# A gated complex recurrence and a low-rank mixer: every engine's order taken from a list plan, blocks of 8 scaled to a middle token, the angle carried by a one-row DMA

## The chip, the cores and the metric

The kernel runs on one core of one Trainium2 chip. The metric is the device time of one execution in microseconds (us); lower is better. The engines are TensorE (PE, with its weight loads as PEld), VectorE (DVE), ScalarE (ACT), GpSimd (POOL), and SyncE (SP), which only starts transfers here.

## The reference

Inputs are q, k, v, a_re, a_im of shape (4 batches, 8 heads, 768 tokens, 48). Cut to what matters:

```python
mag = sqrt(a_re**2 + a_im**2); scale = minimum(mag, 0.999) / (mag + 1e-6)
for t in range(S):                       # complex state S_re, S_im: 48 x 48 per head
    new_re = ar*S_re - ai*S_im ; new_im = ar*S_im + ai*S_re
    S_re, S_im = new_re + outer(k[t], v[t]), new_im
    y[t] = q[t] @ S_re
x  = y as (batch, token, head*48 = 384)
u  = x + (x^T @ U @ V)^T                 # U: 768 x 32, V: 32 x 768, mixes tokens of one batch
out = u + relu(u @ w_ch1) @ w_ch2        # 384 -> 1536 -> 384
```

The gate of a token is a complex number per channel. The kernel keeps its magnitude as a logarithm and its angle as a number of turns. A product of gates over a range of tokens is then the exponential of a sum of logarithms, with a rotation by the sum of angles. U, V, w_ch1 and w_ch2 arrive as 64-bit floats.

## The kernel before

Each batch is cut into 6 chunks of 128 tokens (24 chunks in all, i = 0 to 23). The recurrence of a chunk becomes matrix products, and a 96 x 48 state `G` per head goes from chunk to chunk. The work of a chunk has four parts.

- **Gates** (`gate_steps`, for groups of one chunk, one chunk, and then two chunks each). ACT and DVE compute the logarithm `l` and the turns `y` in wide steps, with two ACT table loads in a group (L281, L323). PE sums them with constant 0/1 matrices: `es` (L301, matrix `after`) is the sum from a token to the end of its block of 4 tokens, `tot` (L314) has the totals of blocks of 4 to 128 tokens, and `ph` (L336) is the running angle of the chunk. The angle at the end of the chunk before is added by a second matmul into the same `ph` tile (L338), whose matrix `tail` picks the last row of `F`. `F` (L339, L340) is the angle with whole turns taken off. The temporaries have one buffer each, so the groups follow one another.
- **Prep** (`prep_steps`): q and k are scaled by `es`, rotated by `cs` (DVE), transposed by PE (`turn`, L380) and copied by ACT to `QK` (L382).
- **Chain** (`chain_steps`): the scores of a chunk are built from small blocks to large ones. `inner(n, hf)` (L417) makes 64 small matmuls inside blocks of 32 tokens, and a masked DVE copy (L421) keeps the pairs that belong to level n. `grow(hf)` multiplies q of each upper half and k of each lower half by the block's total, in place in `QK` (the DVE row of L256, 96 x 1024). `upper` is a half-size step of that kind. There are four `inner` steps: n = 5 (in a block of 4), n = 2 (4 to 8), n = 1 (8 to 16), n = 0 (16 to 32). Then follow `place`, `corners`, `corner`, `keys`, `outputs`, `state` and `rows_of_y` (L507 writes the chunk's x).
- **Mixer** (`mixer_steps`, 12 of them, two chunks each): `rank` (L548) needs all six x tiles of a batch, and with it no mixer can start before the last chunk of its batch. Then come `mixed` and `uT` (L558 to L564), twelve `up` steps (L571, relu by ACT) and two `down` steps (L579), a DVE add (L582) and the store, started by POOL (L583). The tiles `uT` and `h` have one buffer, x has eight.

The weights are turned from 64 to 32 bits by seven DVE steps for each piece (`single`, L211 to L221), 13 pieces.

The order before comes from the program: `weave` spreads several streams of steps evenly over a chunk's iteration: the end of the chain of chunk i-1, the levels of chunk i, the prep of chunk i+1, the gates of a later group, weight pieces, and a share of the mixer steps of earlier batches. Only ACT's table users (`tact`) and a few weight steps are tied to one another by extra edges (`behind`). The last batch's three mixers run one after another at the end:

```python
    weave((0.0, 1.0, rest), (0.0, 1.0, first[done:]))
    for m in range((NT - NCH) // MC, NT // MC):
        run(mixer_steps(m, pu))
```

Of the kernel before, what the change touches and what calls it, by code (L numbers as in the profile page):

```python
# [24 lines left out]
def weave(*streams):  # L25
    order = []
    for si, (begin, end, steps) in enumerate(streams):
        n = len(steps)
        for i, step in enumerate(steps):
            order.append((begin + (end - begin) * (i + 0.5) / n, si, i, step))  # L30
    for _, _, _, step in sorted(order, key=lambda e: e[:3]):
        step()
# [3 lines left out]
def kernel(  # L36
# [39 lines left out]
    M2LO, M2HI = 1e-16, 2.0 ** 62  # L76
# [7 lines left out]
    NTOT = FIRST[CH] + 1  # L84

    def pool(name, bufs, **kw):
        return ctx.enter_context(tc.tile_pool(name=name, bufs=bufs, **kw))

    singles = pool("singles", 1)
    pa = pool("pa", 1)  # L90
    pt = pool("pt", 1)
    pg = pool("pg", 2)
    pqk = pool("pqk", 2)
    pks = pool("pks", 1)
    pkc = pool("pkc", 1)
    pe = pool("pe", 3)
    pTT = pool("pTT", 6)
    pQK = pool("pQK", 3)
    pG = pool("pG", 2)
    py = pool("py", 1)  # L100
    px = pool("px", 8)
    psT = pool("psT", 2, space=PSUM)
    psA = pool("psA", 2, space=PSUM)
    psY = pool("psY", 2, space=PSUM)
    psM = pool("psM", 2, space=PSUM)

    T = {}
# [8 lines left out]
    def load_a(g):  # L116
        lo, hi = GROUPS[g]
        for nm, src in (("ar", a_re), ("ai", a_im)):
            t = pa.tile([128, GC, H, D], FP, tag=nm, name=nm)
            for i in range(lo, hi):  # L120
                nc.sync.dma_start(out=t[:, i - lo], in_=rows(src, i))
            T[nm, g] = t.rearrange("p c h d -> p (c h d)")[:, 0:(hi - lo) * DM]

    def load_qkv(i):
        T["qk", i] = pqk.tile([128, 2, H, D], FP, tag="qk", name="qk")
        for u, src in enumerate((q, k)):
            nc.sync.dma_start(out=T["qk", i][:, u], in_=rows(src, i))
        nc.sync.dma_start(out=VP[i % 4][:, :, 0:D], in_=rows(v, i))

    load_a(0)  # L130

    prefix = singles.tile([128, CH], FP, name="prefix")
    nc.sync.dma_start(out=prefix, in_=spans[:, PRE * CH:(PRE + 1) * CH])
    mask = singles.tile([128, 6, BLK], I32, name="mask")
    nc.sync.dma_start(out=mask, in_=masks)
    ident = singles.tile([128, 128], FP, name="ident")
    make_identity(nc, ident)
    quarter = singles.tile([128, 1], FP, name="quarter")
    nc.vector.memset(quarter, math.pi / 2)
    def column(nm, value):  # L140
# [5 lines left out]
    magic, fourth = column("magic", MAGIC), column("fourth", 0.25)  # L146

    tail = singles.tile([128, CH], FP, name="tail")
    nc.gpsimd.tensor_scalar(out=tail, in0=ident[:, 127:128].to_broadcast([128, CH]), scalar1=-1.0, scalar2=None,
                            op0=OP.mult)  # L150

    after = singles.tile([128, CH], FP, name="after")
    quads = prefix.rearrange("p (b t) -> p b t", t=4)
    nc.gpsimd.tensor_tensor(out=after.rearrange("p (b t) -> p b t", t=4),
                            in0=quads[:, :, 3:4].to_broadcast([128, CH // 4, 4]), in1=quads, op=OP.subtract)
    total = singles.tile([128, NTOT], FP, name="total")
    for n in SIZES:
        o, m, ends = FIRST[n], CH // n, prefix.rearrange("p (b t) -> p b t", t=n)[:, :, n - 1]
        nc.gpsimd.tensor_copy(out=total[:, o:o + 1], in_=ends[:, 0:1])
        if m > 1:  # L160
            nc.gpsimd.tensor_tensor(out=total[:, o + 1:o + m], in0=ends[:, 1:m], in1=ends[:, 0:m - 1], op=OP.subtract)

    for n in (3, 4):
        nc.vector.tensor_tensor(out=mask[:, 5], in0=mask[:, 5], in1=mask[:, n], op=OP.bitwise_or)
    F = singles.tile([128, GC, DM], FP, name="F")
# [10 lines left out]
    load_qkv(0)  # L176
    w1 = singles.tile([128, KD, FF], FP, name="w1")
    w2 = singles.tile([128, KF, DM], FP, name="w2")

    UV = singles.tile([128, 2 * NCH * R], FP, name="UV")  # L180
    U = UV[:, 0:NCH * R].rearrange("p (c r) -> p c r", r=R)

    V = singles.tile([128, S], FP, name="V")
    NP = 128 // R
    WP = 768

    def behind(ins, first):

        tc.add_manual_dep(ins.ins, first.ins.name, mybir.DependencyInfo(
            mybir.DependencyClass.NoSync, mybir.DependencyReason.DATA), reason="order")  # L190

    def single(st, o, pieces):


        n = o.shape[1]
        at = 0
        if pieces[0].dtype == FP:
            for i in pieces:
                nc.sync.dma_start(out=o[:, at:at + i.shape[1]], in_=i)
                at += i.shape[1]  # L200
            return
        raw = st[0].tile([128, WP, 2], U32, tag="raw", name="raw")[:, 0:n]
        for i in pieces:
            m = i.shape[1]
            nc.sync.dma_start(out=raw[:, at:at + m], in_=i.bitcast(U32).rearrange("p (m two) -> p m two", two=2))
            at += m
        lo, hi = raw[:, :, 0], raw[:, :, 1]
        x = st[1].tile([128, WP], U32, tag="x", name="cx")[:, 0:n]
        b = o.bitcast(U32)

        ins = nc.vector.tensor_scalar(out=x, in0=hi, scalar1=0x7FFFFFFF, scalar2=None, op0=OP.bitwise_and)  # L211
        if "level" in T:
            behind(ins, T["level"])
        xf = x.bitcast(FP)
        nc.vector.tensor_scalar(out=xf, in0=xf, scalar1=2.0 ** -15, scalar2=None, op0=OP.max)
        nc.vector.tensor_scalar(out=x, in0=x, scalar1=0x07FFFFFF, scalar2=3, op0=OP.bitwise_and,
                                op1=OP.logical_shift_left)
        nc.vector.scalar_tensor_tensor(out=b, in0=hi, scalar=0xC0000000, in1=x, op0=OP.bitwise_and, op1=OP.bitwise_or)
        nc.vector.tensor_scalar(out=x, in0=b, scalar1=0xFF800000, scalar2=None, op0=OP.bitwise_and)
        nc.vector.scalar_tensor_tensor(out=xf, in0=lo, scalar=2.0 ** -52, in1=xf, op0=OP.mult, op1=OP.mult)  # L220
        nc.vector.tensor_tensor(out=o, in0=o, in1=xf, op=OP.add)  # L221

    def weight_steps(st):
        def small():
            m = R * S // 128
            single(st, UV, [moe_U[c * 128:(c + 1) * 128] for c in range(NCH)] +
                   [moe_V.rearrange("r (s m) -> (r s) m", m=m)])
            for n in range(NP):
                nc.sync.dma_start(out=V[n * R:(n + 1) * R].rearrange("r (s m) -> r s m", m=m), in_=UV[:, NCH * R:])

        first, second = [small], []
        for m in range(0, FF, WP):
            for f in range(KD):
                (second if m else first).append(lambda f=f, m=m: single(
                    st, w1[:, f, m:m + WP], [moe_w_ch1[f * 128:(f + 1) * 128, m:m + WP]]))
        for f in range(0, KF, 2):
            second.append(lambda f=f: single(st, w2[:, f:f + 2].rearrange("p f m -> p (f m)"),
                                             [moe_w_ch2[e * 128:(e + 1) * 128] for e in (f, f + 1)]))
        return first, second

    def act(o, i, f, **kw):
        return nc.scalar.activation(out=o, in_=i, func=f, **kw)  # L242

    queued = []

    def queue(ins):

        if queued:
            behind(ins, queued[-1])
        queued[:] = [ins]  # L250

    def tact(*a, **kw):
        queue(act(*a, **kw))

    def mul(o, a, b):
        nc.vector.tensor_tensor(out=o, in0=a, in1=b, op=OP.mult)  # L256

    def heads(a):
        return a.rearrange("p (x d) -> p x d", d=D)

    def gate_steps(g):
        st = {}
        lo, hi = GROUPS[g]
        W = (hi - lo) * DM

        def tmp(nm):
            st[nm] = pt.tile([128, GC * DM], FP, tag=nm, name=nm)[:, 0:W]  # L270
            return st[nm]

        def s0():
            x, y = tmp("x"), tmp("y")
            act(x, T["ar", g], AF.Square)
            act(y, T["ai", g], AF.Square)
            nc.vector.tensor_tensor(out=x, in0=x, in1=y, op=OP.add)
            nc.vector.tensor_scalar(out=x, in0=x, scalar1=M2LO, scalar2=M2HI, op0=OP.max, op1=OP.min)
# [27 lines left out]
        def of_blocks(i):  # L306
# [3 lines left out]
            if g == 0:  # L310
                queue(nc.scalar.preload_act_table_set("natural_log_exp_and_others"))
# [288 lines left out]
    def run(steps):  # L600
        for f in steps:
            f()
# [97 lines left out]
```

## Time and profile before

| | |
|---|---|
| median of 3 runs | 874.59 us (873.63 to 874.9) |
| the profiled execution, its own time | 874.89 us |
| span of the profiled execution | 873.1 us |
| granted TensorE clock, mean | 0.96 |
| busy: PE / PEld / DVE / ACT / POOL | 788.9 / 585.5 / 426.0 / 464.7 / 37.7 us |

The span runs from the first to the last instruction; the profiled execution's own time is 1.8 us longer. Busy times are unions over the span. A matmul in fp32 appears as two instructions, and matmuls overlap, so the sum over PE's groups is above PE's busy time. The line L256 is the helper `mul`, which many steps use: its rows are told apart by their tiles and shapes.

### The profile page before, as it was taken

Reading aid. Unit: us, or ns where it says so; the run is one execution under the profiler, and the core shown is the slowest. Engines: PE = TensorE matmul, PEld = TensorE weight load, DVE = VectorE, ACT = ScalarE, POOL = GpSimd, SP = SyncE. Lnnn points to the kernel's source line nnn. Section 1 sums busy time; section 2 is a strip of 40 time slices with the busy share of each in tenths; the row PEclk is TensorE's granted clock in tenths of the full one; section 3 lists DMA queues with packets and bytes.
Section 4 is the critical chain, followed back from the end, with each engine's and each line's share of the span. In section 5 each row is a group of like instructions: output and inputs, shape, how many; then the busy total and the mean of one; then the engine's idle time right before and its main releaser. Section 6 shows DMA issues by size and latency. Waiting matters only on the chain.

```text
span 873.1 us, 24512 instructions
## 1 busy us (share of the span) xinstructions
PE 788.9 (90%) x11088; PEld 585.5 (67%) x11088; DVE 426.0 (49%) x621; ACT 464.7 (53%) x983; POOL 37.7 (4%) x67
## 2 busy tenths in 40 slices
PE   3657878878999999999999999999999999999997
PEld 2444656756767876866867867856868778576774
DVE  3577778798965635425526517417516343101010
ACT  7797887476754745736727729619614324020110
POOL 3000000010000000000000000000000000000000
PEclk9977989698799999999999999999999999999999
DMA  7431334243411401301301302301100000000000
GB/s 170 110 92 34 86 75 93 74 99 112 101 20 29 84 11 30 73 20 30 65 11 38 66 10 47 63 23 21 29 19 12 3 20 2 19 1 18 10 10 18
DMA packets 130904, 40.27 MB, mean 46 GB/s; under 512 B 126448, under 2 KB 127344, under 8 KB 130800
## 3 DMA queue, kind: packets, MB, share of 16 engines
q1 hardware_dynamic: 129264, 33.99, 17.6%
q0 software_dynamic: 1536, 4.72, 1.5%
q8 instruction: 87, 1.43, 0.7%
q14 instruction: 17, 0.14, 0.1%
HBM read 33.59 MB, written 4.72 MB: 44 GB/s over the span
## 4 chain that ended last, share of the span: by engine, by line
PE 71%; ACT 19%; DVE 5%; issue 3%; DMA 1%; POOL 1%; POOLq 0%; DVEq 0%; ACTq 0%
PE down L579 21%; PE up L571 18%; PE inner L417 5%; PE tot L314 4%; PE yT L473 4%; PE tr L380 3%; PE ph L336 2%; PE yT L477 2%; PE dk L493 2%; ACT y L242 2%; PE es L301 2%; ACT x L242 2%; ACT cs L242 2%; PE ks L487 2%; ACT AT L445 2%
## 5 line engine op out<-in xcount | busy, mean ns | idle before, releaser
L571 PE MATMUL up<-uT,w 128*128 128x256 f32 x864 | 211.8, 391 | 5.8 <-DVE uT L564 3.4
L579 PE MATMUL down<-w,h 128*128 128x384 f32 x576 | 190.2, 487 | 0.0
L256 DVE TENSOR_TENSOR QK<-QK,T 96x1024 f32<-96x1024 f32 (+1 forms) x144 | 157.1, 1095 | 49.4 <-PE corners L451 33.1
L571 PEld LDWEIGHTS up<-uT,w 128*128 128x128 f32 x864 | 159.8, 193 | 30.3 <-ACT h L242 5.1
L579 PEld LDWEIGHTS down<-w,h 128*128 128x128 f32 x576 | 108.1, 190 | 71.3 <-issue 0.2
L582 DVE TENSOR_TENSOR x<-down,x 128x384 f32<-128x384 f32 x24 | 13.4, 558 | 218.4 <-PE down L579 218.4
L242 ACT ACTIVATE h<-up 128x256 f32<-128x256 f32 x144 | 55.1, 383 | 118.6 <-PE up L571 118.1
L382 ACT COPY QK<-tr 96x512 f32<-96x512 f32 x96 | 55.6, 581 | 72.3 <-PE tr L380 71.4
L417 PEld LDWEIGHTS inner<-QK 96*32 96x32 f32 x6144 | 67.1, 114 | 33.0 <-issue 17.0
L417 PE MATMUL inner<-QK 96*32 96x16 f32 (+1 forms) x6144 | 79.5, 192 | 8.0 <-ACT AT L454 2.9
L380 PE MATMUL tr<-ident,qkc 128*96 128x128 f32 x384 | 63.2, 294 | 12.0 <-DVE qkc L256 10.8
L380 PEld LDWEIGHTS tr<-ident,qkc 128*96 128x96 f32 x384 | 43.9, 134 | 27.6 <-DVE qkc L256 8.8
L480 ACT COPY yTs<-yT 128x512 f32<-128x512 f32 x24 | 14.1, 586 | 82.7 <-PE yT L477 81.3
L421 DVE COPY_PREDICATED DG<-mask,inner 128x256 f32<-128x256 int32 (+1 forms) x96 | 31.6, 329 | 46.1 <-PE inner L417 44.8
L473 PE MATMUL yT<-AT,VP 128*64 128x128 f32 x384 | 46.6, 302 | 5.6 <-ACT AT L465 4.1
L256 DVE TENSOR_TENSOR qkc<-qk,cs 128x768 f32<-128x768 f32 x48 | 44.3, 947 | 2.3 <-PE tr L380 1.6
L445 ACT COPY AT<-DG 32x256 f32<-32x256 f32 x96 | 38.5, 401 | 9.6 <-DVE DG L421 8.7
L314 PEld LDWEIGHTS tot<-total,ll 128*96 128x96 f32 x384 | 37.8, 174 | 6.8 <-ACT ll L309 2.6
L314 PE MATMUL tot<-total,ll 128*96 128x63 f32 x384 | 39.2, 258 | 3.3 <-ACT ll L309 2.0
L473 PEld LDWEIGHTS yT<-AT,VP 128*64 128x64 f32 x384 | 29.6, 149 | 14.2 <-issue 8.1
L301 PE MATMUL es<-l,after 128*128 128x384 f32 x48 | 24.7, 606 | 14.5 <-DVE l L291 12.7
L477 PE MATMUL yT<-QK,G 96*48 96x128 f32 x320 | 37.6, 295 | 0.0
(93 smaller groups left out, 931.4 us busy)
## 6 DMA issues: line engine op xcount, KB each, us to landing
ar<-in_a_re_dram SPq DMA_DIRECT2D x24, 192.0 KB, 3.1
ai<-in_a_im_dram SPq DMA_DIRECT2D x24, 192.0 KB, 3.4
qk<-in_q_dram SPq DMA_DIRECT2D x24, 192.0 KB, 2.9
qk<-in_k_dram SPq DMA_DIRECT2D x24, 192.0 KB, 3.5
VP<-in_v_dram SPq DMA_DIRECT2D x24, 192.0 KB, 2.6
raw<-in_moe_w_ch_dram SPq DMA_DIRECT2D x6, 768.0 KB, 4.8
raw<-in_moe_w_ch_dram SPq DMA_DIRECT2D x12, 384.0 KB, 3.5
out_dram<-x POOLq DMA_DIRECT2D x24, 192.0 KB, 2.1
```

Source lines behind the costliest of these rows:

```text
L242: return nc.scalar.activation(out=o, in_=i, func=f, **kw)
L256: nc.vector.tensor_tensor(out=o, in0=a, in1=b, op=OP.mult)
L301: nc.tensor.matmul(out=ps, lhsT=after, rhs=st["l"][:, (i - lo) * DM:(i - lo + 1) * DM], start=True, stop=True)
L314: nc.tensor.matmul(out=ps[0:D2, h, 0:NTOT], lhsT=ll[:, h].rearrange("p u d -> p (u d)"), rhs=total, start=True, stop=True)
L380: nc.tensor.transpose(out=ps[0:D2, j], in_=T["qkc", i][:, u, hh * HH + j].rearrange("p u d -> p (u d)"), identity=ident)
L382: nc.scalar.copy(out=T["QK", i][:, u, hh * HH:(hh + 1) * HH], in_=ps[0:D2])
L417: nc.tensor.matmul(out=ps[js, h], lhsT=k_of(h)[:, js], rhs=part(q_of(h)[:, js], "p"), start=True, stop=True, tile_position=(0, j * BLK))
L445: nc.scalar.copy(out=AT[i % 2][js, :, js], in_=DG[i % 2][js])
L473: nc.tensor.matmul(out=y[u * DP:(u + 1) * DP, p], lhsT=vv[:, h], rhs=AT[i % 2][:, h], start=True, stop=(c == 0), tile_position=(0, u * DP))
L477: nc.tensor.matmul(out=y[u * DP:u * DP + D, p], lhsT=T["G"][:, h], rhs=q_of(h), start=False, stop=True, tile_position=(0, u * DP))
L571: nc.tensor.matmul(out=ps, lhsT=w1[:, f, ff * 128:(ff + 1) * 128], rhs=st["uT"][:, f], start=(f == 0), stop=(f == KD - 1))
L579: nc.tensor.matmul(out=ps, lhsT=st["h"][:, ff, cc * CH:(cc + 1) * CH], rhs=w2[:, ff], start=(ff == 0), stop=(ff == KF - 1))
```

## The change

Three things change together.

1. **The order.** Steps no longer run when they are written. Each one is given to a `Plan` with its engine, an estimated cost, a rank, what it reads and what it writes. `Plan.order()` simulates the five engines: whenever an engine is free, it takes the ready step with the lowest rank whose buffers are to be had. The instructions are then issued in that order, and at the end every instruction is tied behind the one before it on its engine. The edges order and do not signal. PE steps are handed over in smaller pieces: `inner`, `tot`, `outputs`, `dk` in two, `down` in six of four instructions. Ranks are chunk numbers with offsets; `up` and `down` stand last on PE (100 + m), while the other mixer steps and the ACT and DVE work of the mixers stand first (-5). `rank`, `mixed` and `uT` take their PSUM buffers from the pool of `es`, `tot`, `ph`, `tr` now.
2. **Blocks of 8.** `es` is scaled to the fourth token of a block of 8 (matrix `mid` in place of `after`), so the pairs of a whole block of 8 come from one `inner` step. The step n = 2 goes, with its masked copy. `grow(4)` and the half-size `upper` become two full-size multiplications (`times`).
3. **The angle carry.** The matmul with `tail` goes. POOL starts a DMA that adds the last row of the earlier `F` to the first row of `y`, before the `ph` matmul. `F` has two buffers for groups now, and the sign of `F` is turned.

The core of the diff (the weights, loads, gates' wide steps and mixer steps are the same operations, given to the plan):

```diff
-def weave(*streams):
+class Plan:
+    def add(self, engine, cost, rank, f, reads=(), writes=(), late=0.0):
+        ...   # needs: the earlier steps that touch the same tiles, one of them as a writer
+    def order(self):
+        ...
+            for e in free:
+                kept = []
+                while free[e] <= now and ready[e]:
+                    r = heapq.heappop(ready[e])      # lowest rank first
+                    n = r[1]
+                    if not fits(n):                  # no buffer free for its tiles
+                        kept.append(r)
+                        continue
+                    ...
+                    free[e] = now + ops[n][1]
+                    heapq.heappush(events, (free[e], n, 0))
+                    heapq.heappush(events, (free[e] + ops[n][2] + self.lag, n, 1))
+    plan = Plan(0.06)
+    def c_act(n):
+        return 0.22 + 0.0008 * n
+    def c_dve(n):
+        return 0.15 + 0.00104 * n
+    def SP(*a, **kw):
+        plan.add("SP", *a, late=2.0, **kw)
...
+        POOL(0.5, -7, lambda: nc.gpsimd.tensor_tensor(
+            out=mid..., in0=e[:, :, 3:4].to_broadcast([128, CH // 8, 8]), in1=e, op=OP.subtract), ...)
...
-            if not first:
-                nc.tensor.matmul(out=ps, lhsT=tail, rhs=F[:, (i - 1) % GC], start=False, stop=True)
+            if where(i)[1] > 0:
+                POOL(0.55, R2, lambda: nc.gpsimd.dma_start(out=of(y, i)[0:1], in_=fo(i - 1)[CH - 1:CH], accum_op=OP.add),
+                     [("F", group_of(i - 1), i - 1)], [yi], late=1.6)
...
-        add(inner, 5, 2)
-        add(grow, 4)
-        add(inner, 2, 4)
-        add(upper)
-        for n, hf in ((1, 8), (0, 16)):
-            add(inner, n, hf)
-            add(grow, hf)
-        add(place)
+        inner(5, 2)
+        times(RL, 4, 16, 8, H * CH - 8, 0)
+        inner(1, 8)
+        times(RL, 4, 16, 0, H * CH + 8, 2)
+        grow(RL, 8)
+        inner(0, 16)
+        ...   # the four copies of place
+        grow(RR, 16)
...
+    # ranks: gates lo - 1.6 and lo - 1.5 (lo: first chunk of the group), prep i - 0.8, levels i, rest of the chain i + 0.5,
+    # weight pieces 0.6 to 9.0 and their loads 1.5 below, mixers -5, their up and down on PE 100 + m
...
+            PE(1.3, RM, products, [uT] + [("w1", f, lo) for f in range(KD)], [ps])          # up
+            ACT(0.39, R0, lambda: act(get(*h)[:, ff], get(*ps), AF.Relu), [ps], [h + (ff,)])
...
+            for f0 in range(0, KF, 2):
+                PE(1.29, RM, lambda f0=f0: products(f0), [h + (f0,), h + (f0 + 1,), ("w2", f0)], [ps])   # down
...
+    for n in plan.order():
+        plan.ops[n][4]()
+    last = {}
+    for ins in nc.cur_bb.bb.instructions:
+        if ins.engine in last:
+            tc.add_manual_dep(ins, last[ins.engine], mybir.DependencyInfo(
+                mybir.DependencyClass.NoSync, mybir.DependencyReason.DATA), reason="order")
+        last[ins.engine] = ins.name
```

More of the change, by code (lines that the diff above doesn't have):

```diff
@@ L1 @@
+import heapq
 import math
@@ new lines, in c_one, with c_dma, PE, ACT @@
+    def c_one(n):
+        return 0.15 + 0.00052 * n
+    def c_dma(n):
+        return n * 512 / 170e3
+    def PE(*a, **kw):
+        plan.add("PE", *a, **kw)
+    def ACT(*a, **kw):
+        plan.add("ACT", *a, **kw)
+    def DVE(*a, **kw):
+        plan.add("DVE", *a, **kw)
+    def POOL(*a, **kw):
+        plan.add("POOL", *a, **kw)
+    def SP(*a, **kw):
+        plan.add("SP", *a, late=2.0, **kw)
+    TABLE = ("table", 0)
+    def table(cost, rank, f, reads=(), writes=()):
+        ACT(cost, rank, f, reads=reads, writes=list(writes) + [TABLE])
@@ L145 @@
     leps, lmax, tiny = column("leps", math.log(1e-6)), column("lmax", LNMAX), column("tiny", 1e-30)
[L146 to L165, printed above, removed]
+    magic, fourth, quarter = column("magic", MAGIC), column("fourth", 0.25), column("quarter", math.pi / 2)
+    ident = singles.tile([128, 128], FP, name="ident")
+    make_identity(nc, ident)
     AT, DG, VP = [], [], []
@@ L241, in act @@
[L241 to L265, printed above, removed]
+        buffer(("raw", p), "raw", 2, [128, WP, 2])
@@ L266, in gate_steps, with gates @@
+    def gates(g):
         lo, hi = GROUPS[g]
         W = (hi - lo) * DM
[L269 to L278, printed above, removed]
@@ new lines, in grow @@
+        def grow(rank, hf, u0=0, u1=2):
+            times(rank, hf, 2 * hf, hf, H * CH - hf, 0, u0, u1)
+        inner(5, 2)
[4 more added lines that the diff above has]
+        inner(0, 16)
+        for j in range(CH // BLK):
+            js = slice(j * BLK, (j + 1) * BLK)
+            ACT(0.4, RR, lambda js=js: nc.scalar.copy(out=get(*ATi)[js, :, js], in_=get(*DGi)[js]), [DGi], [ATi + (("d", js.start),)])
+        grow(RR, 16)
@@ L456, in corner @@
+        for r in (0, 64):
+            ACT(0.36, RR, lambda r=r: nc.scalar.copy(out=get(*ATi)[r:r + BLK, :, r + BLK:r + 2 * BLK], in_=get(*ps1)[r:r + BLK]),
+                [ps1], [ATi + (("c", r),)])
+        grow(RR, 32)
+        ps2 = ("corner", i)
+        psum(ps2, "A", [128, HH, 64], [128, H, 64])
         def corner():
[L457 removed]
             for p in range(HH):
@@ L585, in mixer_steps, with turn @@
-        if c0 == 0:
-            add(rank)
+            u = ("xo", i)
+            ps = out_of("mixed", i, [128, DM], [128, 512])
+            PE(0.7, R0, lambda: nc.tensor.matmul(out=get(*ps), lhsT=V[:, c * CH:(c + 1) * CH], rhs=get(*r), start=True, stop=True),
+               [r, ("V", 0), uT + ("kept",)], [ps])
+            DVE(c_dve(DM), R0, lambda: add(get(*u), get(*ps), get(*u)), [ps], [u])
+            tr = out_of("uTp", i, [128, KD, CH], [128, 4, CH])
+            def turn():
+                for f in range(KD):
+                    nc.tensor.transpose(out=get(*tr)[:, f], in_=get(*u)[:, f * 128:(f + 1) * 128], identity=ident)
@@ L587, in mixer_steps @@
         for cc in range(MC):
-            add(mixed, cc)
+            mixed(cc)
         for ff in range(KF):
-            add(up, ff)
+            up(ff)
         for cc in range(MC):
-            add(down, cc)
-        return steps
-    def group_of(i):
-        return next(g for g in range(NG) if GROUPS[g][0] <= i < GROUPS[g][1])
-    def run(steps):
-        for f in steps:
-            f()
-    gates = {g: gate_steps(g) for g in range(NG)}
-    run(gates[0][0] + gates[0][1])
-    load_a(1)
@@ L650 @@
-    weave((0.0, 1.0, rest), (0.0, 1.0, first[done:]))
-    for m in range((NT - NCH) // MC, NT // MC):
-        run(mixer_steps(m, pu))
+            down(cc)
+    constants()
+    weights()
+    for g in range(NG):
+        load_a(g)
+        gates(g)
+        for i in range(*GROUPS[g]):
+            load_qkv(i)
+            prep(i)
+            chain(i)
+            if where(i)[1] == NCH - 1:
+                for m in range(i // MC - NCH // MC + 1, i // MC + 1):
+                    mixer(m)
+    for n in plan.order():
+        plan.ops[n][4]()
```

777 lines of the change are left out of this document (433 added, 344 removed).

## The prediction

> **What bounds the kernel now.** I read the page from the top: busy times, then the slices, because a mean over 873 us mixes stages.
>
> ```profile
> span 873.1 us, 24512 instructions
> PE 788.9 (90%) x11088; PEld 585.5 (67%) x11088; DVE 426.0 (49%) x621; ACT 464.7 (53%) x983; POOL 37.7 (4%) x67
> PE   3657878878999999999999999999999999999997
> DVE  3577778798965635425526517417516343101010
> ACT  7797887476754745736727729619614324020110
> ```
>
> A slice is 21.8 us. In the first ten PE has holes and no other engine is full; after that PE is full and the rest wait for it. To put dates on the stages I take the row of `rank`, and the chain of work that ended last.
>
> ```profile
> L548 PE MATMUL rank<-x,UV x12: 486/510/849, 86.3 to 187.0; 128*32 128x384 f32 x12
> 202.59 6.34 PE up L571 x14
> 398.20 1.31 PE rank L548 x12
> 586.89 1.31 PE rank L548 x12
> 758.69 1.46 PE rank L548 x12
> 765.31 15.81 PE up L571 x72
> 781.12 15.48 PE down L579 x48
> 801.00 15.81 PE up L571 x72
> 836.74 15.81 PE up L571 x72
> ```
>
> The first batch's `rank` ends at 187 and the first `up` starts at 202.6. Stage 1 (to 202.6) is attention with no mixer to fill PE. Stage 2 (to 758.7) has the other 18 chunks and nine mixers, the ranks 188.7 us apart. Stage 3 is the last rank and three mixers, one by one. The busy time of each engine in these stretches (PE, PEld, DVE, ACT, POOL; then granted clock and DMA share):
>
> ```profile
> 0.00:24.00 24.00, 8.80 (x32) 5.88 (x32) 7.73 (x20) 18.05 (x35) 8.33 (x27) 1.00 0.76 169
> 24.00:86.00 62.00, 39.90 (x766) 28.47 (x766) 42.03 (x64) 49.71 (x95) 0.00 (x0) 0.83 0.33 76
> 86.00:187.00 101.00, 83.48 (x1710) 63.41 (x1710) 79.14 (x111) 73.30 (x150) 0.00 (x0) 0.85 0.35 84
> 187.00:202.60 15.60, 11.06 (x253) 7.94 (x251) 14.68 (x25) 12.34 (x31) 2.24 (x2) 0.98 0.53 121
> 202.60:758.70 556.10, 543.00 (x7932) 407.55 (x7936) 272.19 (x386) 296.48 (x639) 23.38 (x31) 0.99 0.16 36
> 758.70:765.30 6.60, 4.06 (x22) 1.52 (x22) 2.38 (x5) 0.96 (x2) 0.54 (x1) 1.00 0.08 30
> ```
>
> In stage 1 up to 187, ACT is busy 141.1 of 187 us (18.05 + 49.71 + 73.30) and DVE 128.9: both about three quarters, each waiting in turn for the other and for PE. So stage 1 is bound by the order of a long dependent chain, on ACT and DVE first. In stage 2 PE is busy for 543.0 of 556.1 us: bound by the amount of PE work. Stage 3 is PE work with gaps.
>
> **The change part by part.** The sum is made against the profiled execution: span 873.1, its own time 874.89, 1.8 around it; the median of the runs is 874.59, so nothing is to be corrected.
>
> *Blocks of 8, on PE.* One `inner` step of four goes in every chunk. Its price is from start to start where PE is full, not the mean of one instruction, since these overlap. The same for `tail`:
>
> ```profile
> 512.83 0.74 PE L417 MATMUL inner<-QK 96*32 96x16 f32 x64
> 513.50 0.64 PE L380 MATMUL tr<-ident,qkc 128*96 128x128 f32 x4
> 524.47 0.81 PE L338 MATMUL ph<-F,tail 128*128 128x384 f32 x2
> 525.12 0.38 PE L493 MATMUL dk<-VP,ks 128*96 128x48 f32 x3
> L417 PE MATMUL inner<-QK 96*32 96x16 f32 (+1 forms) x4352 | 54.1, 189 | 1.1 <-ACT ks L488 0.8
> L338 PE MATMUL ph<-F,tail 128*128 128x384 f32 x28 | 11.3, 486 | 0.0
> ```
>
> An inner step costs 513.50 - 512.83 = 0.67 us, a tail pair 525.12 - 524.47 = 0.65. The last two rows are the counts after 202.6: 4352 / (4 x 64) = 17 chunks lose a step, 17 x 0.67 = 11.4 us; 28 / 2 = 14 pairs go, 9.1 us. PE is full there, so all **20.5 us** come off the end. The other 7 and 6 lie in stage 1, where PE is not the limit; they count in its term.
>
> *Blocks of 8, on DVE.* The masked copy and the half-size multiplication go, one full multiplication comes:
>
> ```profile
> L256 DVE TENSOR_TENSOR QK<-QK,T 96x1024 f32<-96x1024 f32 x112 | 135.3, 1213 | 46.4 <-PE corners L451 33.1 <-PE corner L461 13.3
> L256 DVE TENSOR_TENSOR QK<-QK,T 96x512 f32<-96x512 f32 x32 | 21.8, 680 | 3.0 <-PE corner L461 3.0
> L421 DVE COPY_PREDICATED DG<-mask,inner 128x128 f32<-128x128 int32 x72 | 21.1, 294 | 31.5 <-PE inner L417 30.1
> ```
>
> 1.213 - 0.680 - 0.294 = +0.24 us a chunk. In stage 2 the full PE hides it (DVE is busy 272 of 556 us). In stage 1 it is +1.4 us over six chunks on the engine that then limits, and is in its term. The matrices `mid` and `after` cost POOL the same.
>
> *The carry.* The DMA stands between `F` of one chunk and `ph` of the next. Its nearest rows are POOL's other DMAs and the slowest kinds from SP:
>
> ```profile
> L583 POOL DMA_DIRECT2D out_dram<-x x24 | 13.2, 550 | 424.5 <-DVE x L582 227.7 <-ACT QK L382 153.2 <-issue 25.3
> out_dram<-x POOLq DMA_DIRECT2D x24, 192.0 KB, 2.1
> qk<-in_k_dram SPq DMA_DIRECT2D x24, 192.0 KB, 3.5
> ```
>
> POOL spends 0.55 us on an issue, and a store lands 2.1 us after. An accumulating row of 1.5 KB is not in the trace: less than the store because it is small, more because it reads its target first. I take the store's time, the same queue, and keep 3.5 as the upper end. The chain from angle to angle grows by 0.55 + 2.1 - 0.65 = 2.0 us, 20 times. In stage 2 the lead of the gates (1.5 chunks) and the mixer steps of PE hide it; if that cover is gone, it is 14 x 2.0 = 28 us. But the plan counts 0.55 + 1.6 + 0.06 us where the rows say up to 2.65, and `ph` has a rank ahead of the mixers, so PE can stand at `ph` by up to 0.44 us: 14 x 0.44 = 6 at most. As filler pieces last up to 1.3 us, most waits fall inside one: I take **+2 us**. On POOL the carry queues behind a `ll` copy or a store that waits for DVE; behind a waiting carry stand `ll` and the next store, which have slack: `tot` needs `ll` only a chunk later, and x has eight buffers.
> The Trainium skill (SBUF — State Buffer, on the "DVE blocks DMA" trap) speaks against this step: while DVE runs an instruction in a two-port mode, GpSimd cannot write the descriptors of its DMAs, and one that took about 620 ns alone took about 3100. By that page a carry would be 2.5 us later wherever it meets such an instruction, at most 14 x 2.5 = 35 us in stage 2, an estimate; the row of 2.1 us, a median taken beside a busy DVE, does not show it.
>
> *The order, stage 1.* Rank order finishes the first batch before it works ahead, and mixer steps come first on ACT and DVE, so the 15.6 us between `rank` and the first `up` shrink: the chain there is one copy of the rank and then the same steps that take 4.4 us before an `up` in stage 3 (below), some 5 us in all. How much earlier `rank` comes is bounded from both sides. Lower end: three quarters of use remain, 0 gained. Upper end: DVE, 129 + 1.4 us of work to 187, runs without a hole from 24 on: 24 + (130.4 - 7.7) = 147 and some 5 us of a last chain, 152, a gain of 35. I take 88% use: 24 + 122.7 / 0.88 = 163, with the last chain 168, **19 us** gained. After it, of the 15.6 us some 10 go, but PE was busy for 11.06 of 15.6 us in that stretch with attention work that is only moved, so 10 x (1 - 0.71) = 3; and 3 from shorter `ph` and `inner` there. Stage 1: **-25 us**, range 0 to -45.
>
> *The order, stage 2.* PE's idle time there is 556.1 - 543.0 = 13.1 us. With mixer pieces as a filler of lowest rank nearly all of it can go; but mixers cut in more pieces hand over more often, and that costs:
>
> ```profile
> 355.49 1.49 PE up L571 x6
> 366.70 1.35 PE up L571 x6
> ```
>
> Six `up` instructions in a row take 15.81 / 12 = 1.32 us, and up to 1.49 between attention steps. I take -12 for idle time. With the +2 of the carry: **-10 us**. Range: +8 (90 more cuts of `down`, half of them at 0.17) to -30, since steps stretched that way are a few us in each of the nine mixer periods.
>
> *The order, stage 3.* The last rank falls under mixers of batch 2, and `mixed` and `uT` of the next mixer run while `down` of the one before still computes. From the chain again:
>
> ```profile
> 796.60 0.66 PE mixed L558 x2
> 797.28 0.57 DVE x L560
> 799.80 0.56 PE uT L563 x3
> ```
>
> The gap from 796.60 to 801.00 is 4.4 us, of which 2 x (0.66 + 0.56) = 2.4 are PE work that stays: 2.0 saved, twice. Of the 6.6 us from rank to `up`, the rank's 1.46 and 2.4 stay: 2.7 saved. Together **-7 us**; the last add and store remain.
>
> *What I cost at nothing.* Edges signal nothing. SP's order: a weight load waits for its raw buffer, and behind it stand the loads of a, q, k, v, with a lead of two to three chunks (some 40 us) for a landing of 3.5. The mixers' `mixed` in the pool of `tr` and `tot`: DVE and ACT empty such a tile in half a us.
>
> Sum: 873.1 - 20.5 - 25 - 10 - 7 = 810.6, and 1.8 around it: **812 us**, 7% faster.
>
> **The rivals.**
> - *Stage 1 is not shortened.* Its groups are serial (one set of temporaries), and the carry lengthens five of its links by 2 us. For it: ACT and DVE were at three quarters with a hand-made order too. Against: that order held `up` back by 15 us and worked ahead. Time: 812 + 25 = 837, or 847 if the five carries show.
> - *The carry is late.* At 3.5 us landing, and no cover in half the chunks, 10 x (0.55 + 3.5 - 0.65) = 34: 846. Against: q0 carries little.
> - *Stage 2 fills too.* All stretched steps go and stage 1 comes near DVE's limit: 812 - 15 (of stage 2) - 18 (of stage 1) = 779.
> - *PE waits in fixed order (slower).* Each PE step of attention that needs ACT or DVE, some 15 a chunk, stands at its planned place; where the real handover is later than planned, PE waits with a mixer step behind it that was ready. Waits of that sort after 202.6 (total, times, longest):
>
> ```profile
> PE uT L563 <- DVE x L560: 5.1, 8, 0.7
> PE tr L380 <- DVE qkc L256: 4.4, 7, 2.7
> ```
>
> They last 0.63 us each. There are 18 x 15 = 270 places. Then the 12 us of idle time aren't saved, 824, and (874.6 - 824) / 0.63 = 80 such waits bring it back to the time of before; with 120 it is 900. Against: a ready step comes after a filler of up to 1.3 us, so a lag of 0.2 rarely shows.
>
> **How the numbers follow.** Chances: the forecast (785 to 830) 0.57; stage 2 fills too, 0.10; stage 1 not shortened, 0.13; late carries, 0.07; fixed-order waits, 0.10; gains eaten to within the bound, 0.03. So faster by over 0.2% 0.87 (the first four), the same 0.03, slower 0.10; 0.2% is about what a measurement of this kernel can tell. The range reaches from 772 (nearly all of the better case) to 856 (both middle cases) and leaves out the slower case and a few hundredths below. The forecast's own range is 785 to 830.
>
> **What would show it.** Right: the first `rank` ends near 168 and the first `up` starts within 6 us; `inner` has 4608 matmuls and L338 is gone; ranks some 180 us apart; the last mixers follow one another within 2 us; PE idle below 6 us in stage 2. Wrong: `ph` waiting for a DMA in the list of waits; hundreds of short PE waits for DVE and ACT after the first batch; a first `rank` later than 180.

## The result, and the profile after

| | before | changed |
|---|---|---|
| median | 874.11 us (4 runs) | 815.91 us (810.75 to 818.31, 4 runs) |
| the profiled execution, its own time | 874.89 us | 817.71 us |
| its span; granted TensorE clock, mean | 873.1 us; 0.96 | 815.9 us; 0.94 |

The ratio is 0.933, 95% interval 0.928 to 0.938: 58 us faster. In what follows, one execution of the kernel with the edges on ACT alone, of 985.68 us at a granted clock of 0.733, is left out of its median. The page of the changed kernel begins so:

```profile
span 815.9 us, 21434 instructions
PE 743.5 (91%) x9512; PEld 564.7 (69%) x9512; DVE 447.2 (55%) x622; ACT 468.7 (57%) x983; POOL 55.9 (7%) x89
PE   2556786779999999999999999999999999999996
PEclk9767666898999999999999999999999999999999
```

PE's holes are in the first nine slices now, not ten, and behind them there is none until the last slice. The granted clock in the holes is lower than before. The first `rank` and the first `up` (the two rows of the lines' own view), and from the chain of work that ended last the third and fourth rank and the last mixers:

```profile
L735 PE MATMUL rank<-xo,UV x48: 486/486/510, 179.3 to 682.3; 128*32 128x384 f32 x48
L765 PE MATMUL up<-uT,w x864: 379/379/483, 191.2 to 793.9; 128*128 128x256 f32 x173
534.90 1.42 PE rank L735 x12
681.34 1.42 PE rank L735 x12
682.75 11.85 PE up L765 x54
712.26 15.54 PE up L765 x72
732.61 12.90 PE down L776 x40
745.51 15.54 PE up L765 x72
```

The first `up` starts at 191.2 (202.6 before). The last rank ends at 682.76 and an `up` follows at once; the `down` of one mixer ends at 745.51 and the next `up` starts at 745.51, where there were 4.4 us. The last batch's attention ends 77 us earlier than before and leaves three mixers and three quarters of the `up` steps of a fourth (54 of 72), where three were left before. Busy time by stretch (PE, PEld, DVE, ACT, POOL, clock, DMA share):

```profile
24.00:86.00 62.00, 38.47 (x645) 29.35 (x645) 52.47 (x78) 45.83 (x93) 2.50 (x3) 0.69 0.45 110
86.00:179.30 93.30, 71.55 (x1351) 57.99 (x1347) 76.75 (x104) 70.27 (x139) 2.37 (x3) 0.75 0.34 80
179.30:191.20 11.90, 8.96 (x36) 4.58 (x35) 9.89 (x15) 10.18 (x15) 0.00 (x0) 0.71 0.37 101
191.20:681.30 490.10, 489.04 (x6964) 375.96 (x6963) 286.63 (x382) 308.41 (x661) 38.81 (x46) 1.00 0.18 39
681.30:815.90 134.60, 128.35 (x505) 91.78 (x504) 11.09 (x20) 18.15 (x47) 4.32 (x8) 0.99 0.03 12
```

From 191.2 to 681.3 PE is idle for 1.1 us, with attention and mixers both waiting for it. Up to 191.2 it is busy 126.1 us (with the 7.1 before 24) and idle 65.1; before, it was busy 143.2 and idle 59.4 up to 202.6. So of the span's 57.2 us, 11.4 lie ahead of the first `up` and 45.8 behind it, and the idle time of the first batch has not shrunk.

### The profile page after: what moved, and what is told of

Read it like the earlier page. It is cut to its first block, busy times and chain, and to the rows that moved or that the text cites. A ratio compares the mean times of both kernels' runs of the same rounds, so it can differ in the third digit from the quotient of the medians.

```text
span 815.9 us, 21434 instructions
## 1 busy us (share of the span) xinstructions
PE 743.5 (91%) x9512; PEld 564.7 (69%) x9512; DVE 447.2 (55%) x622; ACT 468.7 (57%) x983; POOL 55.9 (7%) x89
## 4 chain that ended last, share of the span: by engine, by line
PE 82%; DVE 6%; ACT 5%; issue 3%; DMA 3%; POOL 0%; POOLq 0%; ACTq 0%; DVEq 0%
PE up L765 23%; PE down L776 22%; PE tr L551 5%; PE inner L585 5%; PE tot L467 4%; PE dk L695 3%; PE yT L681 3%; PE es ps L450 3%; PE ph L511 2%; PE yT L685 2%; PE mixed L747 2%; PE ks ps L667 2%; DVE QK L248 2%; PE corners L632 2%; DMA y<-F 1%
## 5 line engine op out<-in xcount | busy, mean ns | idle before, releaser
L765 PE MATMUL up<-uT,w 128*128 128x256 f32 x864 | 201.8, 384 | 0.0
L248 DVE TENSOR_TENSOR QK<-QK,T 96x1024 f32<-96x1024 f32 (+1 forms) x144 | 172.8, 1206 | 24.0 <-PE corners L632 16.7
L245 ACT ACTIVATE h<-up 128x256 f32<-128x256 f32 x144 | 55.2, 383 | 147.6 <-PE up L765 146.7
L585 PEld LDWEIGHTS inner<-QK 96*32 96x32 f32 x4608 | 48.2, 112 | 28.6 <-issue 18.1
L251 DVE TENSOR_TENSOR xo<-down,xo 128x384 f32<-128x384 f32 x24 | 13.4, 556 | 97.4 <-PE down L776 97.0
L585 PE MATMUL inner<-QK 96*32 96x16 f32 (+1 forms) x4608 | 55.6, 192 | 11.1 <-DVE QK L248 10.7
L551 PEld LDWEIGHTS tr<-ident,qkc 128*96 128x96 f32 x384 | 44.5, 136 | 25.4 <-DVE qkc L248 13.6
L248 DVE TENSOR_TENSOR qkc<-qk,cs 128x768 f32<-128x768 f32 x48 | 44.1, 956 | 28.4 <-PE tr L551 21.9
L251 DVE TENSOR_TENSOR xo<-mixed,xo 128x384 f32<-128x384 f32 x24 | 13.3, 556 | 81.7 <-PE mixed L747 80.8
L450 PE MATMUL es ps<-l,mid 128*128 128x384 f32 x48 | 24.4, 635 | 19.4 <-DVE l L440 19.4
L782 POOL DMA_DIRECT2D out_dram<-xo x24 | 13.6, 565 | 333.3 <-DVE xo L251 325.9
L712 ACT COPY xo<-yr 128x384 f32<-128x384 f32 x24 | 11.4, 476 | 43.0 <-DMA out_dram<-xo 39.2
L514 DVE SCALAR_TENSOR_TENSOR F<-F,ph 128x384 f32<-128x384 f32 x24 | 13.3, 554 | 41.1 <-ACT F L245 41.1
```

Source lines behind the costliest of these rows:

```text
L251: nc.vector.tensor_tensor(out=o, in0=a, in1=b, op=OP.add)
L450: PE(0.65, R1, lambda: nc.tensor.matmul(out=get(*ps), lhsT=mid, rhs=of(l, i), start=True, stop=True), [l, ("mid", 0)], [ps, ("sums", g, i)])
L551: nc.tensor.transpose(out=get(*ps)[0:D2, j], in_=get(*qkc)[:, u, hh * HH + j].rearrange("p u d -> p (u d)"), identity=ident)
L585: nc.tensor.matmul(out=get(*ps)[js, h], lhsT=k_of(h)[:, js], rhs=part(q_of(h)[:, js], "p"), start=True, stop=True, tile_position=(0, j * BLK))
L765: nc.tensor.matmul(out=get(*ps), lhsT=w1[:, f, ff * 128:(ff + 1) * 128], rhs=get(*uT)[:, f], start=(f == 0), stop=(f == KD - 1))
```

## The experiments

All are edits of the changed kernel, except the third. Medians; the interval is that of the ratio to the kernel before on the same chip.

**Each arithmetic change undone, and the order undone.** The carry by matmul again:

```diff
-            if where(i)[1] > 0:
-                POOL(0.55, R2, lambda: nc.gpsimd.dma_start(out=of(y, i)[0:1], in_=fo(i - 1)[CH - 1:CH], accum_op=OP.add), ...)
+            if not first:
+                PE(0.65, R2, lambda: nc.tensor.matmul(out=get(*ps), lhsT=tail, rhs=fo(i - 1), start=False, stop=True), ...)
```

> The changed kernel with the angle carried by a second matmul again (20 pairs, 14 of them where PE is full). If the carry's DMA is a cost on the chain of the first batch (it holds 11 us of that chain: pieces of 5.66, 1.82 and 3.65 us), stage 1 gets some 5 to 8 us shorter and stage 2 gains 9 us of PE work: 816 to 821. If the DMA is hidden everywhere, only the PE work comes back: 825 or more. If the DMA costs more than the matmul, below 814.

817.94 us (0.932 to 0.939): no difference to 0.933, as the first of the expectations has it. The row of its first `up`, and its stages:

```profile
L768 PE MATMUL up<-uT,w x864: 376/379/483, 183.0 to 794.9; 128*128 128x256 f32 x173
0.00:86.00 86.00, 47.56 (x658) 34.80 (x660) 64.40 (x105) 65.26 (x128) 8.09 (x30) 0.90 0.51 124
86.00:183.00 97.00, 76.63 (x1412) 59.58 (x1408) 82.20 (x113) 78.39 (x151) 0.00 (x0) 0.84 0.37 89
183.00:682.40 499.40, 498.32 (x6986) 380.40 (x6990) 290.33 (x386) 309.46 (x660) 27.03 (x32) 1.00 0.18 38
682.40:815.90 133.50, 128.27 (x504) 91.69 (x501) 11.09 (x20) 18.09 (x47) 4.32 (x8) 0.99 0.03 12
```

The first batch is done 8.2 us earlier (183.0 against 191.2), and behind the first `up` PE has 9.2 us more work (498.32 + 128.27 against 489.04 + 128.35). What is gained ahead of the first `up` is spent behind it. That the 8.2 us are all the DMA's is not shown: the granted clock of this trace is higher too, 0.90 up to 86 us and 0.84 behind it, against 0.78 and 0.75 in the changed kernel.

Blocks of 4 again:

```diff
-        times(RL, 4, 16, 8, H * CH - 8, 0)
-        inner(1, 8)
-        times(RL, 4, 16, 0, H * CH + 8, 2)
+        times(RL, 4, 8, 0, H * CH, 0)
+        inner(2, 4)
+        times(RL, 8, 8, 4, 0, 0, 0, 1)
+        inner(1, 8)
...   # mid, total, mask and inner go back to blocks of 4 as well
```

> The changed kernel with blocks of 4 again: the fourth inner step, its masked copy and the half-size multiplication back, one full multiplication less. If the step's worth is its PE time where PE is full, 18 x 0.67 = 12 us more, and about 0 in the first batch: 828. If the shorter chain of levels also mattered in the first batch: 835 or more. If hidden: 816.

846.72 us (0.967 to 0.971): 31 us slower. That is the number of the second expectation, but not for its reason. The first `up` starts at 194.6, only 3.4 us later. Behind it (the last row is that of the changed kernel, from 191.2 on):

```profile
194.60:709.40 514.80, 505.09 (x8112) 387.72 (x8114) 279.64 (x397) 307.11 (x659) 36.95 (x46) 1.00 0.17 36
709.40:843.90 134.50, 128.27 (x504) 91.70 (x503) 11.09 (x20) 18.10 (x47) 4.32 (x8) 0.99 0.03 12
L585 PE MATMUL inner<-QK 96*32 96x16 f32 (+1 forms) x4608 | 54.1, 189 | 7.9 <-issue 6.9 <-PE up L766 0.8
L585 PE MATMUL inner<-QK 96*32 96x16 f32 (+1 forms) x3456 | 40.5, 190 | 0.0
```

649.3 us against 624.7: 24.6 more, or 1.37 us for each of 18 chunks. PE's busy time is 16.0 us longer (505.09 + 128.27 against 489.04 + 128.35; the two rows of `inner` differ by 13.6), and it is idle for 8.6 us more. 6.9 of these stand ahead of `inner` steps and are put down to issue, time in which PE waited for nothing that the profile shows. In the list order the step of 64 short matmuls costs more than its 0.67 us.

The kernel before, in its old order, with blocks of 8 and the carry by DMA (the same formulas, written into `gate_steps` and `chain_steps`):

> The kernel before, in its old order, with the two changes of the arithmetic alone (blocks of 8 and the carry by DMA). If PE work is what they save, 874 - 20 = 854, and the order then is worth the other 38. If waits in the old order swallow the saving (the DMA stands in the way of ph), 865 to 874. If the order is worth little, near 820.

858.82 us (0.979 to 0.985): the arithmetic alone gives 15.7 us on that chip, and the order the other 43. Its stages:

```profile
198.40:738.50 540.10, 523.74 (x6816) 392.93 (x6820) 283.73 (x372) 294.71 (x642) 38.39 (x45) 0.99 0.16 36
738.50:854.00 115.50, 102.72 (x403) 72.24 (x402) 10.22 (x19) 14.75 (x38) 3.78 (x7) 0.99 0.03 12
```

From the first `up` on it takes 655.6 us, the changed kernel 624.7; its idle time there is 29.1 us against 7.3. The first `up` differs by 7 us (198.4 and 191.2). PE's busy time behind the first `up` is 626.5 us, 19.2 less than before the change (645.7). The parts do not add up: with blocks of 4 kept, the order and the carry bring 27.8 us (874.53 - 846.72 on that chip), with the old order kept, the blocks and the carry bring 15.7, and all together 58.

**The edges.** Without the loop that ties each instruction to the one before it, and with it on ACT alone:

```diff
-        if ins.engine in last:
+        if ins.engine in last and ins.engine == mybir.EngineType.Activation:   # the second; the first has no loop
```

> The changed kernel without the edges that tie each instruction to the one before it on its engine; the steps are still issued in the plan's order. If the issue order alone sets each engine's order, nothing moves: 816. If the instructions are reordered again without the edges, the plan is lost in part: 830 to 870, with PE waits after the first batch.

889.93 us (1.015 to 1.020), slower than the kernel before. ACT shows why:

```profile
L245 ACT ACT_TABLE_LOAD x84 | 107.8, 1283 | 1.4
L242 ACT ACT_TABLE_LOAD x27 | 34.6, 1283 | 1.1 <-PEq L838 0.7
```

The 27 loads are the kernel's own, as many as in the changed kernel. The 84 others stand at the helper of the functions (L245), where the changed kernel has none: functions of two tables were mixed on ACT.

> The changed kernel with the ordering edges on ACT alone. Without any edge it took 890, with 84 more table loads on ACT of 1.28 us. If these loads are the whole of that loss, 816 to 820. If the order of PE, DVE and the queues also needs edges, 830 to 870.

830.16 us, the median of three (0.945 to 0.954). So of the 74 us that the edges are worth, about 60 are the order on ACT, and 14 that of the other engines. No trace shows where the 14 lie.

**What holds the first batch.** Less work on DVE, by leaving out six of the seven conversion steps:

> The changed kernel with one of the seven DVE steps that turn a weight piece from 64 to 32 bits; the other six are left out, the loads stay. DVE loses about 57 us of work, some 45 of it before the first up. If DVE bounds the first batch, the first up comes 25 us earlier or more: 790. If ACT and the chain of dependent steps bound it, 8 us or less: 808 to 816. The carry that landed in 5.7 us beside weight steps on DVE and a weight load on the DMA engines lands in 2 us if DVE was the cause, in 5 if the load was.

821.85 us (0.937 to 0.942): not faster. DVE is busy 394.6 us instead of 447.2, and the first `up` still starts at 193.4. DVE's load is not the bound. The chain of this run has pieces of 4.43 us (from 42.50) and 4.26 us (from 88.20) of the carry; the stretches around these, then a later one of 2.55:

```profile
42.50:47.00 4.50, 3.45 (x25) 2.85 (x25) 0.47 (x1) 2.93 (x7) 0.98 (x1) 0.55 0.70 223
88.20:92.50 4.30, 0.00 (x0) 0.00 (x0) 0.00 (x0) 0.00 (x0) 0.74 (x1) 0.82 0.63 224
137.30:139.80 2.50, 1.83 (x24) 1.52 (x18) 0.60 (x2) 0.59 (x1) 0.73 (x1) 1.00 0.04 7
```

In the second the whole core waits for one row of 1.5 KB while DVE does nothing and the DMA engines are 63% busy with weight loads. A carry is late here without any DVE step beside it.

The gates of chunks 6 and 7 behind the levels of chunk 5:

```diff
-        R1, R2 = lo - 1.6, lo - 1.5
+        R1, R2 = (lo - 0.4, lo - 0.35) if lo == NCH else (lo - 1.6, lo - 1.5)
```

> The changed kernel with the gates of chunks 6 and 7 ranked behind the levels of chunk 5 (5.6 in place of 4.4), so that the first batch ends before work for the second. If work ahead on ACT and DVE holds the first batch up, the first rank comes 8 to 15 us earlier, and the postponed work hides under the mixers: 805 to 810. If the chain bounds the first batch, or PE then lacks chunks 6 and 7, 816 to 822.

813.97 us (0.928 to 0.933). The first `up` starts at 179.5, 11.7 us earlier, and the time hardly moves: the interval meets that of the changed kernel.

```profile
0.00:179.50 179.50, 115.49 (x2035) 90.94 (x2035) 143.21 (x213) 131.38 (x261) 12.04 (x34) 0.78 0.43 106
```

PE is idle for 64.0 us (179.5 - 115.49) ahead of the first `up` here and for 65.1 in the changed kernel. Work that is put off is done later by a full PE: the date of the first `up` is not the gain, PE's idle time is.

The transposes of the first six chunks in the mixers' empty PSUM buffers (`"M" if i < NCH else "T"`):

> The changed kernel with the transposes of the first six chunks in the mixers' two PSUM buffers, which stand empty until the first rank, and not in the two that es, tot, ph and mixed share. If a lack of PSUM buffers lengthens the first batch, the first up comes 5 us earlier or more and the time is 806 to 812. If not, 814 to 818.

819.72 us (0.934 to 0.942): the buffers are not what holds it. The first `up` starts at 188.3, 2.9 us earlier, though the granted clock of this trace is 0.83 from 24 to 86 us and 0.82 from 86 to 180, against 0.69 and 0.75.

PE's clock, by steps that nothing reads, ranked 99. The diff is that of the third version; in the first the steps are ready from the start, in the other two with each chunk's `es`:

```diff
+            for _ in range(14 if i < NCH else 0):
+                PE(0.45, 99.0, warm, [("sums", g, i)], [spare])   # one fp32 matmul, 128 x 256
```

> The changed kernel with 280 added PE steps that nothing reads (two 128 x 128 matmuls each, 0.21 us), behind all attention work and ahead of up and down, so that they fill PE's idle time in the first batch. If PE's low granted clock there (0.69 to 0.75 between 24 and 191 us, against 0.83 to 0.86 before) is what kept stage 1 long, the clock rises to 1.0, es and ph fall from 0.89 to 0.5 us an instruction, and the first up comes 15 to 25 us earlier: near 800. If ACT, DVE and the chain bound it and PE's clock does not, 816 or some us more for added steps in the way.

> The changed kernel with 120 added PE steps that nothing reads, each two fp32 matmuls of 128 x 256 and priced at 0.45 us (the steps tried before took 0.47 us where the plan had 0.21, so they were PE's bound and told nothing of the clock). Twenty become ready with each of the first six chunks, behind attention and ahead of up and down. If PE's low granted clock is what holds the first batch, the clock there rises to about 0.9 or more and the time falls to 800 to 810. If ACT and the chain hold it, the time is 816 to 830, as part of the 54 us added stands in the way.

877.20 us (1.002 to 1.009) and 858.08 us (0.979 to 0.986). Both fillers cost about double their price: the first 133.1 us of PE for 280 steps, 0.475 each against 0.214; the second 0.87 against 0.45, since a step had two matmuls of two instructions. They made PE the bound up to the first `up` (at 249.0 and 233.5) and tell nothing of the clock. They cost about what PE's 65 us of idle time could not take: 133 - 65 = 68 us for 61 measured, and 120 x 0.87 - 65 = 39 for 42. Whether the wrong price did harm of its own is not shown, as no run has the same steps at the right price. The third has one matmul in a step, as priced:

> The changed kernel with 84 added PE steps that nothing reads, 14 ready with each of the first six chunks, each one fp32 matmul of 128 x 256, priced at 0.45 us (two instructions of 0.217 us from start to start). They add 36 us to PE, which is idle for 65 us before the first up. The larger fillers before had cost double their price, so PE became the bound. If the low granted clock holds the first batch, it rises from 0.7 towards 0.9 and the time falls to 805 to 811. If the chain through ACT and DVE holds it, whatever PE's clock, 816 to 825.

810.41 us (0.926 to 0.932), 6 runs. With 36 us of added work the first `up` starts at 182.5, 8.7 us earlier, at a higher clock:

```profile
24.00:86.00 62.00, 47.95 (x735) 38.07 (x734) 54.25 (x81) 45.79 (x94) 2.62 (x3) 0.81 0.44 107
86.00:182.00 96.00, 81.94 (x1429) 65.95 (x1427) 84.12 (x116) 77.06 (x149) 2.53 (x3) 0.89 0.35 88
```

0.81 and 0.89 stand against 0.69 and 0.75. But the clock is not all that differs. The chain of this run holds one piece of the carry ahead of the first `up`:

```profile
81.93 2.94 DMA y<-F
```

That of the changed kernel holds three, of 5.66, 1.82 and 3.65 us, 11.1 together. So 8.2 us less of the chain are carries, and what the clock gave of the 8.7 is open. It is the fastest version that was run, but its interval overlaps with that of the changed kernel, so that a gain of 5 us is likely and not shown.

**The filler.** `up` and `down` ranked first on PE:

```diff
-        R0, RM = -5.0, 100.0 + m
+        R0, RM = -5.0, -5.0
```

> The changed kernel with up and down ranked first on PE (-5) and not last (100 + m). If stage 2 is full because mixer steps fill in behind attention, taking them first starves attention: PE waits for ACT and DVE in stage 2, and the last batch ends later: 835 to 860. If any order that the plan holds fills PE, 812 to 820.

993.89 us (1.130 to 1.143), far beyond the expectation. Its slices of PE and ACT:

```profile
PE   3658768899996767799997797989999687789997
ACT  6885877601236767732115767670221675421110
```

Mixers taken at once leave nothing to fill with: every batch now begins as the first one does, with holes in PE while the chain runs through ACT and DVE (digits of 6 and 7 four times in the row of PE). The granted clock falls to 0.849 in the mean. A full stage 2 comes from holding `up` and `down` back.

## Why the prediction was right

The forecast was 812 us; the profiled execution took 817.71, the median is 815.91, 4 to 6 us more. Of the 62.5 us that the sum takes off the span, 57.2 came, but not where they were put: 11.4 ahead of the first `up` for 25 forecast, and 45.8 behind it for 37.5. That the forecast is off by no more than 6 us is luck: two misses, of 14 and 8 us, nearly cancel.

- **Removed PE work, 20.5 us: right as PE work, and not the whole worth.** In the old order PE's busy time behind the first `up` fell by 19.2 us. In the list order an `inner` step is worth more: with the step put back, the run from the first `up` on grows by 1.37 us a chunk where I had 0.67. I priced it by one start-to-start distance at a place where nothing waited; with four steps a chunk in the list order PE also stands ahead of them waiting for issue. Why it does so there, and neither with three (0.0 us) nor with four in the old order (1.1 us ahead of L417 behind 202.6, most of it for ACT), stays open. The `tail` pairs came off PE as priced, 9.2 us for 9.1, but the carry as a whole brought nothing: the run with the matmul has its first `up` 8.2 us earlier. I had put a longer first batch into a rival (847, "if the five carries show") and not into the stage's value.
- **Stage 1, -25 us: wrong.** The first `up` came 11.4 us earlier, and with `es` and `tot` of two chunks and the levels of one not yet done (16 `es` matmuls ahead of it, 20 before). PE's idle time there rose from 59.4 to 65.1 us. The step that failed is the 88% use of DVE. DVE did get fuller (83% from 24 us to the first `rank`, 74% before) and was not the limit: with 53 us less work for it in the whole kernel the first `up` came at 193.4. Nor were PSUM buffers the limit. The last chain, from the start of `rank` to the first `up`, took 11.9 us and not 5. The measure was wrong too: I counted the date of the first `up` and not PE's idle time ahead of it, and the run with late gates shows that 11.7 us of date can be worth next to nothing.

  What the limit is stays open. Two things moved the first `up` by 8 to 9 us, and no run parts them: the carry (the matmul in its place, but at a higher clock) and PE's granted clock (the last filler, but with 8.2 us less of carries in the chain). I did not think of the clock, though 0.83 and 0.85 stood in the rows that I quoted. PE's three longest waits ahead of the first `up` (total, times, longest) are for steps of DVE:

```profile
PE es ps L450 <- DVE l L440: 19.4, 4, 10.1
PE tr L551 <- DVE qkc L248: 10.8, 4, 4.9
PE inner L585 <- DVE QK L248: 10.7, 6, 2.8
```

  The first is the end of a group's gates, which follow one another as they share one set of temporaries. That serial chain is the candidate that was not tried.
- **Stages 2 and 3, -17 us for waits: as forecast.** Behind the first `up`, PE's idle time fell from 24.8 to 7.3 us, by 17.5. It is PE's busy time that fell by more than forecast, by 28.4 us (645.7 to 617.4) and not 20.5, though more work had been put off into it. Fewer steps stretched by a wait would explain the rest, and so would the granted clock, 0.99 in stage 2 before and 1.00 now; neither is shown. The old order with the new arithmetic puts the order's share behind the first `up` at 31 us. The cover named for it, mixer steps that PE takes last, is what does it: with the mixers first it is gone. The mixers at the end follow one another as forecast.

The signs named ahead come out right behind the first `up` and wrong ahead of it. `inner` has 4608 matmuls, L338 is gone, PE is idle for 1.1 us in stage 2, and the last mixers follow one another at once. But the first `rank` ends at 183.8, not near 168, the first `up` comes 7.4 us behind it, not within 6, and `ph` waits for the carry's DMA there, 4 times and 2.8 us in all: a late `rank` and such waits were named as signs of being wrong. The ranks are 160, 195 and 146 us apart, not evenly 180.

The rivals. PE waits in fixed order: from 191.2 on PE waited for another engine twice:

```profile
PE yr L710 <- ACT xo L712: 0.6, 1, 0.6
PE yT L681 <- DVE G L251: 0.4, 1, 0.4
```

1.0 us, not 80 waits of 0.63. The late carry is real, but only ahead of the first `up`: of the 14 carries behind it none lands later than 2.6 us, and PE waits for none. Its rows, by POOL's groups, by DMA issues and by the line's own view:

```profile
L507 POOL DMA_DIRECT2D y<-F x20 | 16.0, 800 | 286.5 <-ACT y L245 135.5 <-DVE F L514 102.0 <-ACT h L245 34.0
y<-F POOLq DMA_DIRECT2D x20, 1.5 KB, 1.9
DMA to landing us min/median/max: 1.8/1.9/5.7
```

An issue takes 0.80 us (0.55 taken), the landing 1.9 in the median (2.1 taken) and 5.7 at most, beyond my upper end of 3.5. "Stage 1 is not shortened" is what happened in substance; it did not cost the 25 us because more came off behind the first `up` than forecast, as in my third rival. The number was right as a sum of parts of two rivals of opposite sign.

## What to carry to other kernels

Where one engine is the bound in the long run, measure a change by that engine's idle time and by the work it still has to do, not by the date at which a stage ends. A list order pays by keeping a stock of work that the limiting engine takes last, and by edges that hold it on every engine: without them this one was slower than the order by hand, most of it through the order on ACT. Added steps cost what the idle time of that engine cannot take: 36 us of them in 65 us of idle time cost nothing, 133 us cost 61. Before a date in one trace is compared with a date in another, their granted clocks are to be compared.

## What the runs showed of the hardware

- The granted clock of PE is 1.00 where PE is full, and PE's use does not set it alone where it is not. From 24 to 86 us the changed kernel had PE busy 62% and a clock of 0.69, the run with transposes apart 61% and 0.83, the kernel before 64% and 0.83. With the third filler, busy 77% and 85% in the two long stretches, it was 0.81 and 0.89. In the first 24 us of the changed kernel it was 1.00 with PE busy 30%. The four executions of the changed kernel took 810.75, 814.12, 818.31 and 817.71 us at mean clocks of 0.961, 0.957, 0.949 and 0.941. The Trainium skill (TensorE: Matmul & The Clock Gate, Part 1) says that the throttled state is the default and that activity lifts it; the full stretches and the fillers agree, the first 24 us and the spread near 62% do not follow from it alone.
- A one-row DMA from POOL, 1.9 us in the median, takes 4.3 to 5.7 us beside weight loads issued by SP just before. Three stretches of the changed kernel from issue to landing:

```profile
77.64:83.30 5.66, 3.42 (x24) 2.79 (x24) 3.95 (x6) 1.31 (x3) 0.75 (x1) 0.50 0.60 176
126.38:128.20 1.82, 1.12 (x16) 0.94 (x16) 1.82 (x4) 1.35 (x5) 0.75 (x1) 0.50 0.02 1
174.32:177.97 3.65, 3.19 (x30) 2.77 (x28) 3.51 (x6) 0.70 (x2) 0.75 (x1) 0.61 0.03 5
```

  In the first the DMA engines are 60% busy; the run with one conversion step shows the same with DVE idle. In the third they are free and DVE is busy for 3.51 of 3.65 us, three of its five weight steps at 0.55 us for 768 elements and two at 0.96. In the second DVE is busy throughout, with multiplications and one weight step of 0.95 us, and the row lands in 1.82 us. The Trainium skill (SBUF — State Buffer, the "DVE blocks DMA" trap) says that while DVE runs an instruction in a two-port mode, GpSimd cannot write the descriptors of its DMAs. The third stretch may be that; no run here shows the mode of a DVE step, and whether it decides was not tried.
- Leaving ACT's order open added 84 table loads of 1.283 us, 107.8 us of ACT's time.
